# Two-stage attention and a maxout layer on one core: pooling of batch 1 one burst later, first two output pairs with their linear term last

## The chip, the cores and the metric

The kernel runs on one core of a Trainium2 chip. Times are device microseconds (us) of one execution. The profile is one profiled execution on the same core; its engines are PE (TensorE), DVE (VectorE), ACT (ScalarE), POOL (GpSimd) and SP (SyncE, which here only issues DMAs).

## The reference

There are 4 batches of 12544 tokens with 128 channels, 32 inducing rows, and a layer with 1024 hidden columns.

```python
def mab(q, kv):                    # a = softmax(scale * q @ kv.T), returns a @ kv
...
h = mab(I, x)                      # pooling: 32 rows attend to all tokens of a batch
x = mab(x, h)                      # every token attends to the 32 pooled rows
g = np.maximum(x @ w1, x @ w2)
return g @ w_out
```

## The kernel before

The layer is taken apart as max(a, b) = a + relu(b - a). So an output tile is relu(e · hwd) · w_out plus a linear term e · m1, both scaled by the softmax's reciprocal sum. Here e are the unnormalised exponentials of a token against the 32 pooled rows, hwd is the pooled rows times (w2 - w1), and m1 is the pooled rows times w1 · w_out.

**Pooling** of a batch goes over seven pieces of 16 (the last one 2) tiles of 128 tokens. `p1_scores` (line 361) takes 16 matmuls (L366) from the transposed tokens `xT` and one exponential on ACT (L375). `p1_accum` (line 381) takes 16 matmuls (L388), an addition on DVE (L398 for the first, then L401) and one on POOL (L405, then L408). `small_fold`, `small_h`, `small_hwd` and `small_m1` then make hwd and m1 of that batch, and `m1d` (L513, on POOL: m1 masked into four blocks of 32 rows). `transpose_batch` (line 134) lets SP issue seven DMA transposes (L130), released by a tiny POOL copy (L136).

**Bursts** are the main work. `seq` (line 782) lists them over all batches; the loop of line 834 counts them as g. Batch 0 has g = 0 to 48: one block of 8 tiles (4 bursts), five of 16 tiles (8 bursts each), one of 8 (4) and one of 2 (1). A burst (line 586) is eight matmuls (L606) into four PSUM banks; each bank is then evicted with a relu, on DVE (L637) or ACT (L641), as a small planner (`Model.pick`, line 41) decides at build time from assumed costs. There are eight banks in all; `bank` (line 104) takes the one that the planner thinks free first, and the first writer of a bank waits for the eviction that empties it.

**Finals** are the output pairs: 16 matmuls (L668) from the evicted relu tiles, a product with the reciprocal sums on DVE (L694), and after every second one a DMA to the output (L704, issued by POOL for batches 0 to 2). Four finals follow from every part of four bursts, and one is taken from the queue in each iteration. The linear term of a final comes in one of two ways. For two finals at once it goes first, as four matmuls of 32 rows (L621) right behind the burst: that is the `lead`, taken when the queue's head has an even number. Without a lead it goes last, as two matmuls of 128 rows with `m1d` (L677).

The order of every engine is what the loop writes. Within iteration g it is: the burst with its lead, one-time preparations (g = 1 to 3; `small_m1(0)` in g = 3), the staging of later blocks (L541, L551), one final, the sums of a new block (L562, L571), and then the jobs that `at` put down for g, among them the pooling of the next batch:

```python
for i in range(NP1):
    s = g + (14 + 4 * i if b == 0 else 5 + 5 * i)
    at(s, p1_scores, nb, i)
    at(s + 2, p1_accum, nb, i)
```

For batch 1, then, scores stand in g = 14, 18, ..., 38 and sums in g = 16, 20, ..., 40. In batch 0 the leads stand in every even g from 4 on. The rest of the pooling chain stands in g = 40 (fold), 43, 44 and 45.

## Time and profile before

| | |
|---|---|
| median of 5 runs | 341.36 us (339.39 to 342.08) |
| profiled execution, whole time | 339.07 us |
| its span | 337.3 us |
| mean granted TensorE clock | 0.998 |
| busy: PE, DVE, ACT, POOL | 328.0, 298.3, 271.2, 94.1 us |
| L606 (burst) | 1600 matmuls, 81.5 us busy |
| L668 (finals) | 3136 matmuls, 208.6 us busy |
| L621 (lead) | 380 matmuls, 31.2 us busy |
| L637 (relu on DVE) | 337, mean 679 ns |
| L641 (relu on ACT) | 447, mean 601 ns |
| L694 (output product on DVE) | 196, mean 417 ns |

A row with an engine, a line and an operation is a group of like instructions; "busy" is their summed time without overlaps. In the timeline each row gives the start, the time until the last of a run of like instructions ended, the engine, the line, what is written from what, and in brackets how long the engine had been idle and what ended that. Matmuls are pipelined, so one that takes 0.2 us may follow the one before it after 0.06 us: what counts for the path is the distance from start to start. PEld is the loading of weights, which runs ahead of the matmuls.

### The profile page before, as it was taken

How to read it: one execution, taken by the hardware profiler on the slowest of the kernel's cores; microseconds unless marked ns; L12 is line 12 of the kernel's file. 1: busy time of each engine (PE TensorE's matmuls, PEld its weight loads, DVE VectorE, ACT ScalarE, POOL GpSimd, SP SyncE). 2: the span in 40 equal slices, each digit the busy share in tenths (PEclk: the TensorE clock that was granted, in tenths of full speed). 3: DMA queues.
4: the chain of work that ended last, by engine and by line, in shares of the span. 5: the costliest groups of instructions: out<-in, count | busy, mean ns of one | idle time of the engine just before them, and what ended most of it. 6: DMA issues, size and time to landing. Idle time of an engine off the chain costs nothing.

```text
span 337.3 us, 14365 instructions
## 1 busy us (share of the span) xinstructions
PE 328.0 (97%) x6267; PEld 260.3 (77%) x6267; DVE 298.3 (88%) x631; ACT 271.2 (80%) x526; POOL 94.1 (28%) x166
## 2 busy tenths in 40 slices
PE   7988999999999999999999999999999999999995
PEld 3775868887878878888877878888777777878875
DVE  1768989999989999999998999999998998999993
ACT  4658878887898787887898877787899989888881
POOL 6331222356632234542341232332242100000000
PEclk9999999999999999999999999999999999999999
DMA  8999899999629996994219991221221221222222
GB/s 211 208 206 215 214 228 225 250 205 252 179 96 201 213 207 154 199 240 142 89 71 216 224 214 66 95 95 66 96 96 64 111 96 72 94 92 97 95 96 111
DMA packets 54143, 51.47 MB, mean 153 GB/s; under 512 B 41536, under 2 KB 42464, under 8 KB 54080
## 3 DMA queue, kind: packets, MB, share of 16 engines
q0 software_dynamic: 11552, 32.38, 36.5%
q1 hardware_dynamic: 42528, 18.17, 25.4%
q8 instruction: 49, 0.80, 0.9%
q14 instruction: 14, 0.11, 0.1%
HBM read 28.33 MB, written 25.69 MB: 160 GB/s over the span
## 4 chain that ended last, share of the span: by engine, by line
PE 86%; DMA 6%; ACT 3%; DVE 2%; POOL 1%; issue 1%; POOLq 0%
PE ps L668 55%; PE ps L606 18%; PE ps L621 4%; DMA xn<-in_x_dram 4%; ACT relu L641 2%; PE ps L366 2%; PE ps L388 2%; PE ps L541 2%; DMA xT<-xn 2%; DVE relu L637 1%; DVE o L694 1%; POOL xn L126 1%; PE ps L562 1%; ACT e L551 0%; PE ps L482 0%
## 5 line engine op out<-in xcount | busy, mean ns | idle before, releaser
L641 ACT ACTIVATE relu<-ps 128x512 f16<-128x512 f32 x447 | 237.1, 601 | 42.7 <-PE ps L606 30.5
L637 DVE TENSOR_SCALAR relu<-ps 128x512 f16<-128x512 f32 x337 | 217.1, 679 | 6.3 <-PE ps L606 5.1
L668 PE MATMUL ps<-woutp,relu 128*128 128x128 f16 x3136 | 208.6, 220 | 0.0
L668 PEld LDWEIGHTS <-relu 128*128 128x128 f16 x3136 | 175.6, 98 | 31.4 <-issue 21.7
L694 DVE TENSOR_TENSOR o<-ps,rp 128x256 f32<-128x256 f32 x196 | 81.7, 417 | 17.5 <-PE ps L668 13.0
L704 POOL DMA_DIRECT2D out_dram<-o x75 | 41.1, 548 | 149.8 <-DVE o L694 115.7
L606 PE MATMUL ps<-e,hwd 32*128 32x256 f16 (+1 forms) x1600 | 81.5, 270 | 0.7 <-ACT relu L641 0.4
L606 PEld LDWEIGHTS <-hwd 32*128 32x128 f16 x1600 | 26.2, 92 | 18.9 <-issue 3.3
L621 PE MATMUL ps<-m,e 32*128 32x128 f16 x380 | 31.2, 214 | 1.5 <-ACT m L508 0.8
L621 PEld LDWEIGHTS <-e 32*128 32x128 f16 x380 | 18.5, 92 | 9.0 <-issue 6.1
L408 POOL TENSOR_TENSOR eacc<-eacc,et 128x512 f32<-128x512 f32 (+1 forms) x18 | 18.5, 1028 | 0.2
L375 ACT ACTIVATE et<-ps 128x512 f16<-128x512 f32 (+1 forms) x21 | 11.4, 545 | 5.0 <-PE ps L366 5.0
L121 POOL DMA_DIRECT2D xn<-in_x_dram x21 | 11.4, 546 | 4.6 <-DMA xn<-in_x_dram 2.1
L366 PE MATMUL ps<-inducingT,xT 128*128 128x32 f16 x294 | 10.6, 176 | 0.7 <-DMA xT<-xn 0.7
L551 ACT ACTIVATE e<-ps 128x512 f16<-128x512 f32 (+1 forms) x21 | 10.9, 583 | 0.0
L388 PE MATMUL ps<-et,xn 128*128 128x32 f16 x294 | 10.6, 176 | 0.0
L366 PEld LDWEIGHTS <-xT 128*128 128x128 f16 x294 | 9.5, 96 | 0.9 <-issue 0.9
L388 PEld LDWEIGHTS <-xn 128*128 128x128 f16 x294 | 9.4, 96 | 0.0
L541 PE MATMUL ps<-xT,hT 128*32 128x512 f16 (+2 forms) x116 | 8.5, 356 | 0.0
L194 PE MATMUL ps<-warm 128*128 128x512 f16 x21 | 7.0, 483 | 1.2 <-DVE warm L170 1.2
L246 PE MATMUL ps<-identity,xn 128*128 128x128 f16 x98 | 7.0, 219 | 1.0 <-DMA xn<-in_x_dram 0.4
L251 DVE COPY xT<-ps 128x1024 f16<-128x1024 f16 (+2 forms) x11 | 6.2, 593 | 1.5 <-PE ps L246 1.4
(86 smaller groups left out, 116.4 us busy)
## 6 DMA issues: line engine op xcount, KB each, us to landing
out_dram<-o POOLq DMA_DIRECT2D x72, 256.0 KB, 3.3
xn<-in_x_dram POOLq DMA_DIRECT2D x21, 512.0 KB, 8.6
out_dram<-o SPq DMA_DIRECT2D x24, 256.0 KB, 2.0
xf<-in_x_dram SPq DMA_DIRECT2D x2, 512.0 KB, 4.3
wf<-in_moe_w_dram SPq DMA_DIRECT2D x2, 512.0 KB, 5.7
xn<-in_x_dram POOLq DMA_DIRECT2D x3, 256.0 KB, 11.2
out_dram<-o POOLq DMA_DIRECT2D x3, 128.0 KB, 4.2
xT<-xn SPq DMA_TRANSPOSE x21, 6.7
```

The lines of the kernel that those rows point to most:

```text
L121: nc.gpsimd.dma_start(out=xn_of(b, i)[:, 0:n, :], in_=xr[b, :, k0 : k0 + n, :])
L366: nc.tensor.matmul(out=ps[:, j * M : (j + 1) * M], lhsT=xT_tiles[b % 2][:, k0 + j, :], rhs=inducingT, start=True, stop=True,)
L388: nc.tensor.matmul(out=ps[:, 0:M], lhsT=xn[:, j, :], rhs=et[:, j, :], start=(j == 0), stop=(j == n - 1),)
L408: nc.gpsimd.tensor_add(out=acc, in0=acc, in1=et[:, 0:n, :])
L541: nc.tensor.matmul(out=ps[32 * q : 32 * (q + 1), 0 : self.width], lhsT=st[self.b]["hT4"][:, 32 * q : 32 * (q + 1)], rhs=xT[:, q % self.g], ...
L606: nc.tensor.matmul(out=ps[:, jj * w : (jj + 1) * w], lhsT=st[blk.b]["hwd"][r, 128 * jb : 128 * (jb + 1)], rhs=blk.e2[r, 128 * self.t0 : 12 ...
L621: nc.tensor.matmul(out=part.fin[q][1][:, 128 * s : 128 * (s + 1)], lhsT=part.blk.e2[r, 128 * tt : 128 * (tt + 1)], rhs=st[part.blk.b]["m1" ...
L637: nc.vector.tensor_scalar(out=dst, in0=src, scalar1=0.0, scalar2=None, op0=ALU.max)
L641: nc.scalar.activation(out=dst, in_=src, func=AF.Relu)
L668: nc.tensor.matmul(out=o, lhsT=self.relu[:, jb, q, tt, :], rhs=woutp[:, jb, :], start=(start and s == 0 and jb == 0), stop=(not start and ...
L694: nc.vector.tensor_mul(self.osb[:, h : h + 2, :], ps[:, 0:256].rearrange("p (s c) -> p s c", s=2), rp.broadcast_to((128, 2, 128)),)
L704: eng.dma_start(out=outr[blk.b, :, k : k + nst, :], in_=self.osb[:, 0:nst, :])
```

## The change

The pooling of batch 1 (scores, sums, and the additions that they issue on DVE and POOL) moves from g = 14 + 4i to g = 15 + 4i, so to the iterations without a lead. The fold moves by one iteration and the three steps behind it too, to g = 41, 44, 45 and 46. The condition `g > 4` takes away the lead of g = 4, which belonged to the first two finals of the run; these take the linear term last, in L677. The leads of g = 6, 8, ... stay. The inserted line shifts the line numbers behind 835 by one.

```diff
@@ -808,13 +808,13 @@
             if nb + 1 < B:
                 at(g + l0, hold_loads, nb)
             for i in range(NP1):
-                s = g + (14 + 4 * i if b == 0 else 5 + 5 * i)
+                s = g + (15 + 4 * i if b == 0 else 5 + 5 * i)
                 at(s, p1_scores, nb, i)
                 at(s + 2, p1_accum, nb, i)
                 if nb + 1 < B:
                     at(g + l0 + 2 * i, load_x, nb + 1, i)
             d = 1 if b == 0 else 0
-            for s, f in ((40, small_fold), (42 + d, small_h), (43 + d, small_hwd), (44 + d, small_m1)):
+            for s, f in ((40 + d, small_fold), (42 + 2 * d, small_h), (43 + 2 * d, small_hwd), (44 + 2 * d, small_m1)):
                 at(g + s, f, nb)
@@ -833,7 +833,8 @@
         for g, (p, u) in enumerate(seq):
             lead = []
-            if len(queue) > 1 and queue[0][0].tn == 2 and queue[0][1] % 2 == 0:
+
+            if g > 4 and len(queue) > 1 and queue[0][0].tn == 2 and queue[0][1] % 2 == 0:
                 lead = queue[0:2]
             p.burst(u, lead)
             if 1 <= g <= 3:
```

Since the planner counts along, it deals the banks and some relus anew: in the built programs DVE has three relus more and ACT three fewer, all of them in batch 0. Behind the beginning of batch 1 both engines have the same instructions in the same order.

## The prediction

> **What bounds the kernel now.** I read the page first (parts 1 and 4).

> ```profile
> span 337.3 us, 14365 instructions
> PE 328.0 (97%) x6267; PEld 260.3 (77%) x6267; DVE 298.3 (88%) x631; ACT 271.2 (80%) x526; POOL 94.1 (28%) x166
> PE 86%; DMA 6%; ACT 3%; DVE 2%; POOL 1%; issue 1%; POOLq 0%
> ```

> PE carries 86% of the chain that ended last, so a wait of PE costs its length, and an instruction that PE gets rid of its issue distance. Next the list of waits:

> ```profile
> PE ps L621 <- ACT m L508: 0.8, 1, 0.8
> PE ps L366 <- DMA xT<-xn: 0.7, 1, 0.7
> ```

> These are two single waits of PE, and both belong to steps that the change moves. The timeline shows the first in its place:

> ```profile
> 29.21 0.45 ACT L508 ACTIVATE m<-ps,rs 128x128 f16<-128x128 f32 x1
> 29.70 0.29 PE L621 MATMUL ps<-m,e 32*128 32x128 f16 x4 [0.77 <-ACT m L508]
> 29.74 1.18 POOL L513 TENSOR_TENSOR m1d<-m,mask 128x256 f16<-128x256 f16 x2 [6.65 <-ACT m L508]
> 29.92 1.07 PE L668 MATMUL ps<-woutp,relu 128*128 128x128 f16 x16
> 31.00 0.40 PE L606 MATMUL ps<-e,hwd 32*128 32x256 f16 x8
> ```

> It is the lead of g = 4 waiting for m1, which ACT makes behind four relus. A later stretch of the timeline has the second, and a third kind that the list doesn't show:

> ```profile
> 45.81 0.55 PE L366 MATMUL ps<-inducingT,xT 128*128 128x32 f16 x16 [0.73 <-DMA xT<-xn]
> 46.29 0.40 PE L606 MATMUL ps<-e,hwd 32*128 32x256 f16 x8
> 46.40 0.60 ACT L375 ACTIVATE et<-ps 128x512 f16<-128x512 f32 x1 [0.83 <-PE ps L366]
> 46.72 1.29 DVE L637 TENSOR_SCALAR relu<-ps 128x512 f16<-128x512 f32 x2 [1.18 <-PE ps L606]
> 46.89 2.29 ACT L641 ACTIVATE relu<-ps 128x512 f16<-128x512 f32 x4
> 47.62 0.40 PE L606 MATMUL ps<-e,hwd 32*128 32x256 f16 x8
> 47.85 0.44 PE L621 MATMUL ps<-m,e 32*128 32x128 f16 x4
> 47.92 0.42 DVE L694 TENSOR_TENSOR o<-ps,rp 128x256 f32<-128x256 f32 x1
> 48.02 0.09 PEld L621 LDWEIGHTS <-e 32*128 32x128 f16 x2 [0.18 <-issue]
> 48.25 1.28 DVE L637 TENSOR_SCALAR relu<-ps 128x512 f16<-128x512 f32 x2
> ...
> 58.32 0.27 PE L621 MATMUL ps<-m,e 32*128 32x128 f16 x4
> ```

> L366 is the first pooling scores (g = 14), waiting for the first DMA transpose, which landed at 45.67 (the chain has it from 39.45 for 6.22). The third kind is in the lead after each scores. The exponential goes ahead of the burst's relus on ACT; in g = 16 the second bank of the lead is emptied by the second relu behind it, at about 48.0, and the four L621 take 0.44 where others take 0.27. It is the same in g = 20, 24, 28, 32 and 36: 6 × 0.17 = 1.02 us.

> **What is already tight.** From start to start a burst with its final takes 1.33 us, with a lead 1.44 (timeline, 31.0 to 45.0); scores or sums of a full piece add 0.40, the sums of a new block (L562) 0.08, the staging of two blocks (L541) 0.54. Eight bursts of pooling without a wait are 4 × 1.33 + 4 × 1.44 + 4 × 0.40 + 0.08 = 12.76; g = 20 to 28 took 13.07 (54.66 to 67.73), which is these plus two waits of 0.17. The windows show DVE close behind:

> ```profile
> 46.29:59.92 13.63, 13.63 (x287) 10.95 (x286) 12.36 (x26) 11.03 (x21) 3.97 (x6) 1.00 1.15 226
> ```

> (length, then busy time and count of PE, PEld, DVE, ACT, POOL): DVE works 12.36 of 13.63.

> **The lead of g = 4 goes.** Four L621 go and four L677 come; nothing else moves. L668 of g = 4 no longer stands behind m1. In the built program it waits for the third of the four relus that ACT starts at 27.30, which ends near 28.95, so it can run from 29.0 to 30.0. Then L677 waits for m1d: the first of two POOL products (610 ns each, and the wait is for the first alone) ends at 29.74 + 0.61 = 30.35. So a wait is left, 0.4 instead of 0.77, now behind the final. Two L677 cost what two L668 do, 2 × 0.06; then L562 0.08, and burst 5 starts near 30.65 instead of 31.00. In g = 5 two more L677 take 0.12 back: gain 0.23. Bounds: 0.6 if POOL is done sooner than its rough span says, minus 0.4 if PE had to see both products. I take 0.23. Queued behind the wait are L562 and burst 5, whose relus nobody misses in that time (ACT sat idle 0.80 before those of burst 5).

> **The first scores one burst later.** Burst 15 starts at 45.01 instead of 46.29, scores stand behind its final at 46.3, 0.6 after the transpose landed, which has its release (POOL's L136 in g = 9) and SP queue unchanged. The 0.73 and 0.07 of issue around it go: 0.80. What the wait gave was rest for ACT and DVE (DVE was idle 1.18). Followed forward by their own rows, DVE is free at 45.45, just when burst 15 gives it work, and burst 16 finds its banks empty; I count no loss. If the rest was needed, it comes back as waits: bounds 0.80 and 0.3.

> **The other moves.** PE's work is the same. In even g the lead's banks are now emptied by relus of a burst without an exponential ahead: the 1.02 go. But the exponential now stands ahead of the relus of an even burst, and the next burst is only 1.44 (or 1.52 with L562) away. By the rows above, the second relu behind the exponential ends 1.72 after the burst's start (46.29 to 48.01). In g = 21, 29 and 37 the fourth bank of the burst is emptied by just this relu, PE asks for it at 1.52 + 0.13: 0.09 each, 0.27. In g = 17, 25, 33 it is the first relu (1.2): no wait.

> DVE counts more. In the built program it has 16 relus, not 15, in each eight bursts of the pooling, so every burst gives it two relus and an L694. What do they cost? [...] But the rows overlap: two relus take 1.29, so the second adds 0.61, and from 46.72 over 47.92 to 48.25 a pair takes 1.20 and an L694 0.33. Start to start that is 16 × 0.60 + 8 × 0.33 + 2 × 0.29 + 0.16 = 12.98. This is nearer to what the engine did, so I take it: 0.22 above PE's 12.76, still 0.09 under 13.07. The 0.22 show as waits of 0.06 to 0.09 in the lead of every fourth burst and those of g = 21, 29, 37. The stretches with staging give DVE 0.54 of rest. I sum the new waits to 3 × 0.09 + 5 × 0.07 = 0.62; bounds zero and 1.02 (just the old ones again). Net gain of the stretch: 0.40.

> POOL: its additions now stand behind the output DMA of the same odd g; POOL is busy 4 to 7.6 us in each 13 us window, and the fold has as many bursts before `small_h` as before, so nobody waits. The last steps (g = 44 to 48): `small_hwd` now falls together with a staging and three ACT relus. The copy of hwd on ACT still holds PE near 0.5 in g = 46, as now (bursts 46 and 47 are 2.52 apart, 0.5 more than their work), and g = 45 and 48 may wait 0.1 to 0.2 more while `small_h` no longer lengthens g = 43: minus 0.1, bounds ±0.4. L136 for batch 2 stands behind m1d, up to 2 us later; its first scores came 11 us after it, with a transpose taking about 6.7, so that is covered.

> **Sum.** 0.23 + 0.80 + 0.40 - 0.10 = 1.33 us. The profiled execution took 339.07 (span 337.3 and 1.8 around it), so 337.7 for a like one. That execution was 0.7% quicker than the median of the five runs, and I put the same difference on the median: 341.36 - 1.3 = 340.1.

> **The rivals.**
> *No new waits* (0.22): evictions keep up and all of 1.02 goes. 0.23 + 0.80 + 1.02 = 2.05: 339.3, or 338.4 with the upper bounds. For it: ACT gets three relus less, and the new waits are sums of rows good to a few hundredths. Against: DVE's 12.98.
> *The wait is only moved* (0.12): the rest that DVE and ACT lose at 45.8 comes back, and m1d comes too late. Gain 0.2: 341.1.
> *DVE becomes the bound* (0.16), the slower case, in g = 15 to 41: if a relu takes more than 0.60 start to start, every eight bursts grow by 16 times that, 3.4 such stretches. [...]

> **How the numbers follow.** The likeliest case has 0.50; its own range is 339.3 to 340.9. A difference of under 0.5%, 1.7 us, can't be told from no change here, and 1.33 lies under that; I give 3 in 10 of this case to faster. Faster: 0.22 + 0.15 = 0.37; same: 0.35 + 0.12 = 0.47; slower: 0.16. The range goes from the better bound of the first rival, 338.4, to 342.6, which leaves out most of the DVE case and little else.

> **What would show it.** Right: no wait of L621 for L508, a wait of L677 for POOL of some 0.4; no wait of L366 for the transpose; burst 15 near 44.8; L621 after scores 0.27 to 0.35; eight pooling bursts in about 13.0 with DVE busy over 12.5 of them. Wrong: L668 of g = 4 not before 29.5; burst 16 held by DVE; eight bursts of 13.4 or more (then DVE bounds) or of 12.8 (then nothing does but PE); g = 44 to 49 longer by over 0.5.

## The result and the profile after

The kernel after takes 338.42 us (median of 27 runs, 337.84 to 340.42), the kernel before 341.12 (46 runs, 339.15 to 343.31). The ratio is 0.9931, 95% interval 0.9916 to 0.9947, so faster by 0.7%. The profiled execution took 338.12 us with a mean granted clock of 0.999, against 339.07 and 0.998 before. The profiled executions differ by 0.95 us and the medians by 2.70: that gap is the subject of most of what follows.

The page of the kernel after, span, busy engines and first line of the chain that ended last:

```profile
span 336.4 us, 14365 instructions
PE 327.8 (97%) x6267; PEld 261.1 (78%) x6267; DVE 300.0 (89%) x634; ACT 270.1 (80%) x523; POOL 94.0 (28%) x166
PE 89%; DMA 4%; issue 3%; ACT 2%; POOL 1%; DVE 1%; POOLq 0%
```

PE's share of the chain rose from 86% to 89%. In the list of waits (total, times, longest) the two of the prediction's list are gone, and one half as long has come:

```profile
PE ps L677 <- POOL m1d L513: 0.4, 1, 0.4
```

The timeline of the kernel after at the first final:

```profile
28.82 1.05 PE L668 MATMUL ps<-woutp,relu 128*128 128x128 f16 x16
29.07 0.44 ACT L508 ACTIVATE m<-ps,rs 128x128 f16<-128x128 f32 x1
29.60 1.18 POOL L513 TENSOR_TENSOR m1d<-m,mask 128x256 f16<-128x256 f16 x2 [6.81 <-ACT m L508]
30.27 0.27 PE L677 MATMUL ps<-m1d,e 128*128 128x128 f16 x2 [0.39 <-POOL m1d L513]
...
30.55 0.40 PE L606 MATMUL ps<-e,hwd 32*128 32x256 f16 x8
```

L668 now runs while ACT makes m1, at 28.82 instead of 29.92. Further on in the same timeline, the first scores and the burst and lead behind them:

```profile
45.98 0.55 PE L366 MATMUL ps<-inducingT,xT 128*128 128x32 f16 x16
...
46.46 0.40 PE L606 MATMUL ps<-e,hwd 32*128 32x256 f16 x8
46.56 0.60 ACT L375 ACTIVATE et<-ps 128x512 f16<-128x512 f32 x1 [0.35 <-PE ps L366]
...
46.69 0.27 PE L621 MATMUL ps<-m,e 32*128 32x128 f16 x4
```

L366 has no wait in brackets, and the four L621 behind the scores take 0.27, not 0.44. The price is in a burst, g = 21 (the same in g = 29 and 37):

```profile
54.84 0.59 PE L606 MATMUL ps<-e,hwd 32*128 32x256 f16 x8
```

Eight L606 take 0.59 where others take 0.40. The windows of eight bursts, g = 20 to 28, after:

```profile
53.32:66.22 12.90, 12.90 (x279) 10.97 (x277) 12.75 (x28) 9.66 (x18) 2.98 (x5) 1.00 1.09 235
```

and before:

```profile
54.67:67.73 13.06, 13.06 (x279) 10.82 (x278) 12.37 (x27) 10.09 (x20) 5.05 (x8) 1.00 1.05 238
```

DVE works 12.75 of 12.90 us, yet the stretch became 0.16 shorter.

Now all burst starts of the two traces, each counted from the first burst of its own trace (the loading before it differs by 0.13 us from one execution to another). The table gives how much earlier (minus) a burst of each kernel starts than in the profile of before, in us.

| burst g | before, again | after | after, again | lead only | quarters | two later |
|---|---|---|---|---|---|---|
| 5 | 0.00 | -0.32 | -0.32 | -0.31 | -0.54 | -0.32 |
| 14 | 0.00 | -0.20 | -0.20 | -0.20 | -0.42 | -0.20 |
| 16 | 0.16 | -1.03 | -0.96 | 0.13 | -1.31 | -1.49 |
| 28 | 0.17 | -1.38 | -1.30 | 0.13 | -1.66 | -1.46 |
| 42 | 0.16 | -1.58 | -1.51 | 0.18 | -1.86 | -1.16 |
| 51 | 0.17 | -1.34 | -1.27 | 0.19 | -1.62 | -0.80 |
| 57 | 0.17 | -0.81 | -0.19 | 0.19 | -1.62 | -0.81 |
| 69 | 0.17 | -0.80 | -0.18 | 0.20 | -1.61 | -0.80 |

### The profile page after: what moved, and what is told of

It is laid out like the page before. It is cut to its first block, busy times and chain, and to the rows that moved or that the text cites. A ratio compares the mean times of both kernels' runs of the same rounds, so it can differ in the third digit from the quotient of the medians.

```text
span 336.4 us, 14365 instructions
## 1 busy us (share of the span) xinstructions
PE 327.8 (97%) x6267; PEld 261.1 (78%) x6267; DVE 300.0 (89%) x634; ACT 270.1 (80%) x523; POOL 94.0 (28%) x166
## 4 chain that ended last, share of the span: by engine, by line
PE 89%; DMA 4%; issue 3%; ACT 2%; POOL 1%; DVE 1%; POOLq 0%
PE ps L668 57%; PE ps L606 19%; PE ps L621 4%; DMA xn<-in_x_dram 4%; PE ps L366 2%; PE ps L388 2%; PE ps L541 2%; ACT relu L641 1%; POOL xn L126 1%; PE ps L562 1%; DVE o L694 0%; PE ps L246 0%; PE ps L677 0%; PE ps L303 0%; PE ps L482 0%
## 5 line engine op out<-in xcount | busy, mean ns | idle before, releaser
L641 ACT ACTIVATE relu<-ps 128x512 f16<-128x512 f32 x444 | 235.5, 601 | 43.0 <-PE ps L606 30.6
L637 DVE TENSOR_SCALAR relu<-ps 128x512 f16<-128x512 f32 x340 | 218.7, 678 | 4.6 <-PE ps L606 3.6
L668 PE MATMUL ps<-woutp,relu 128*128 128x128 f16 x3136 | 208.8, 220 | 0.4 <-issue 0.4
L668 PEld LDWEIGHTS <-relu 128*128 128x128 f16 x3136 | 175.8, 98 | 31.9 <-issue 22.3
L694 DVE TENSOR_TENSOR o<-ps,rp 128x256 f32<-128x256 f32 x196 | 81.7, 417 | 16.8 <-PE ps L668 11.9
L606 PE MATMUL ps<-e,hwd 32*128 32x256 f16 (+1 forms) x1600 | 82.2, 270 | 0.8 <-ACT relu L641 0.4
L606 PEld LDWEIGHTS <-hwd 32*128 32x128 f16 x1600 | 26.3, 92 | 19.3 <-issue 3.6
L621 PE MATMUL ps<-m,e 32*128 32x128 f16 x376 | 29.8, 214 | 0.6
L621 PEld LDWEIGHTS <-e 32*128 32x128 f16 x376 | 18.4, 92 | 6.7 <-issue 3.5
L375 ACT ACTIVATE et<-ps 128x512 f16<-128x512 f32 (+1 forms) x21 | 11.4, 544 | 5.1 <-PE ps L366 5.1
L366 PE MATMUL ps<-inducingT,xT 128*128 128x32 f16 x294 | 10.6, 176 | 0.0
L366 PEld LDWEIGHTS <-xT 128*128 128x128 f16 x294 | 9.5, 96 | 0.0
L541 PE MATMUL ps<-xT,hT 128*32 128x512 f16 (+2 forms) x116 | 8.5, 356 | 0.2 <-ACT hwd L490 0.2
L513 POOL TENSOR_TENSOR m1d<-m,mask 128x256 f16<-128x256 f16 x8 | 4.7, 608 | 11.0 <-ACT m L508 6.8
```

The lines of the kernel that those rows point to most:

```text
L366: nc.tensor.matmul(out=ps[:, j * M : (j + 1) * M], lhsT=xT_tiles[b % 2][:, k0 + j, :], rhs=inducingT, start=True, stop=True,)
L541: nc.tensor.matmul(out=ps[32 * q : 32 * (q + 1), 0 : self.width], lhsT=st[self.b]["hT4"][:, 32 * q : 32 * (q + 1)], rhs=xT[:, q % self.g], ...
L606: nc.tensor.matmul(out=ps[:, jj * w : (jj + 1) * w], lhsT=st[blk.b]["hwd"][r, 128 * jb : 128 * (jb + 1)], rhs=blk.e2[r, 128 * self.t0 : 12 ...
L621: nc.tensor.matmul(out=part.fin[q][1][:, 128 * s : 128 * (s + 1)], lhsT=part.blk.e2[r, 128 * tt : 128 * (tt + 1)], rhs=st[part.blk.b]["m1" ...
L637: nc.vector.tensor_scalar(out=dst, in0=src, scalar1=0.0, scalar2=None, op0=ALU.max)
L641: nc.scalar.activation(out=dst, in_=src, func=AF.Relu)
```

## The experiments

Two theories stood at first for the difference between 0.95 and 2.70. A: in a typical execution of before the first scores wait longer for the transpose than in its profile. B: pauses without a semaphore fall differently. Both were tested with the kernel before itself, with each half of the change alone, and with an earlier transpose.

**Before, once more** (no edit).

> The kernel before once more, unchanged, for a second look at an execution nearer to its median (341.1) than the profiled one (339.07). Theory A: the gain beyond the 1.3 us that the schedule accounts for is a longer wait for the first DMA transpose. Then an execution of 341 shows PE waiting 2 to 3 us (not 0.7) at the first pooling scores of g = 14, and the rest of its bursts stand as in the first profile. Theory B: it is pauses that no semaphore explains, as the one of 0.4 us in g = 56 of the changed kernel. Then the wait at g = 14 stays near 0.7 and PE has idle time put down to issue, 1.5 to 2.5 us in sum, at places that differ. If it happens to be an execution near 339 it tells neither apart.

Measured: 339.31 us at a granted clock of 1.0; up to burst 69 its bursts stand within 0.17 us of the first profile (0.34 at the end of the run), and it waits 0.89 us for the transpose where that one waited 0.73. So profiles of full clock agree with each other, and not with the median.

**The later pooling alone.**

```diff
-                s = g + (14 + 4 * i if b == 0 else 5 + 5 * i)
+                s = g + (15 + 4 * i if b == 0 else 5 + 5 * i)
...
+            for s, f in ((40 + d, small_fold), (42 + 2 * d, small_h), (43 + 2 * d, small_hwd), (44 + 2 * d, small_m1)):
```

> Only the pooling one burst later; the lead of g = 4 stays. By the steps of the prediction 0.80 + 0.40 - 0.10 = 1.1 us of schedule. Theory A: also the whole surplus of the change's median, so 2.1 us in all, ratio 0.994, times as narrow as those of the changed kernel. Theory B: 1.1 us, ratio 0.997, and a spread like the kernel before.

Measured: 340.44 (11 runs; a twelfth took 346.61 and is left out) against 340.66; ratio 0.9994, 0.9962 to 1.0026. Both theories had foretold a gain. The profiled execution took 341.03 at a mean clock of 0.990. Its windows show where that is lost (the column behind POOL's busy time and count is the granted clock):

```profile
28.00:29.00 1.00, 0.75 (x9) 0.30 (x9) 1.00 (x2) 1.00 (x3) 0.00 (x0) 1.00 1.02 205
29.00:30.00 1.00, 0.28 (x4) 0.12 (x3) 1.00 (x3) 1.00 (x4) 0.24 (x1) 0.64 1.07 217
30.00:32.00 2.00, 2.00 (x27) 1.94 (x28) 0.35 (x2) 0.65 (x2) 0.94 (x2) 0.50 1.09 217
...
36.00:38.00 2.00, 2.00 (x39) 1.58 (x39) 1.34 (x3) 1.56 (x4) 0.00 (x0) 0.97 0.90 216
```

The clock was halved from 29.28 (0.64 in one us means 0.72 us at half) to 36.12 (0.97 in two), so for 6.84 us. It begins inside the wait of the lead of g = 4, and the final behind it is stretched, as the timeline of this kernel shows:

```profile
29.72 0.39 PE L621 MATMUL ps<-m,e 32*128 32x128 f16 x4 [0.77 <-ACT m L508]
30.05 1.89 PE L668 MATMUL ps<-woutp,relu 128*128 128x128 f16 x16
```

Sixteen L668 take 1.89 instead of 1.07; burst 7 stands 2.8 us later than in before. From burst 14 to 42 the pooling then gains 1.44 us, as in after (1.38). Of the 12 runs only two kept a full clock; they took 338.03 and 338.74. This asked for a third theory, **C**: in many executions TensorE's granted clock is halved (0.50 in the windows above) at the start of batch 0, and taking away the lead of g = 4 prevents it.

**The lead alone.**

```diff
-            if len(queue) > 1 and queue[0][0].tn == 2 and queue[0][1] % 2 == 0:
+            if g > 4 and len(queue) > 1 and queue[0][0].tn == 2 and queue[0][1] % 2 == 0:
```

> Only the lead of g = 4 goes; pooling stays in the even bursts. Burst 5 comes 0.3 us earlier and burst 6 some 0.2. Theory A: that 0.2 is swallowed by the wait for the transpose at g = 14, which comes no earlier by it (its release hangs on POOL's queue): 0 to 0.2 us, ratio 0.9995 to 1.0, spread as before. Theory B: 0.2 us, ratio 0.9993.

Measured: 340.13 (12 runs), ratio 0.9978, 0.9954 to 1.0002. In the profile the 0.20 us won are lost at burst 15, to the wait for the transpose (table above). But all 12 runs have a full clock, where before had it in 12 of 29 beside them. **The same kernel once more:**

> The change without the later pooling, looked at once more: its full-clock runs fell in two groups, near 339.2 and between 340.1 and 340.9, and its profile was of the first. If this execution takes 340.1 or more, its burst starts show where the second group loses 1 us: at burst 15 (a longer wait of the first scores for the transpose), or in pauses without a semaphore elsewhere. If it takes 339.2, nothing is learnt of the second group.

Measured: 339.49, nothing learnt of the runs above 340.1. The full-clock runs of this kernel lie 0.7 us above those of before (339.41), and why stays open.

**The transposes two bursts earlier.**

```diff
-            t0, l0 = (9, 24) if b == 0 else (-3, 16)
+            t0, l0 = (7, 24) if b == 0 else (-3, 16)
```

> The kernel before with the transposes of batch 1 asked for in g = 7 instead of g = 9 (SP and POOL otherwise the same). It takes away the wait at g = 14 alone, pooling stays beside the leads, and the 0.17 at the leads behind the scores stay. Theory A: 0.75 us in a quick execution and the whole surplus in the median, so 1.7 to 2.0 us, ratio 0.9945, with a narrow spread. Theory B: 0.75 us, ratio 0.998, spread as before. If the last load of batch 1 lands only after g = 7, POOL waits for it and the gain is smaller in both.

Measured: 339.78, ratio 0.9982, 0.9960 to 1.0003, and in the profile no gain at all: the releasing copy (L136) now waits 1.90 us for the last load of the batch, and L366 still waits 0.81 us at 45.81. Starting later is what removes this wait; the release can't come earlier. Theory A finds no support here. Nine of the 12 runs lost the clock, yet their median is only 0.55 above that of the three that kept it (339.94 against 339.39), so a lost clock hasn't one price. Here the release hangs on a load and not on the bursts, and the wait behind it may have taken up part of the delay; no trace of such a run was kept.

**The runs sorted by their mean granted clock.** All runs of before beside the experiments (102) fall into three groups: 42 at 0.9975 or more, median 339.41; 48 near 0.995, median 341.25; 12 near 0.990, median 341.99. Against the full clock a mean of 0.995 is one stretch of 3.40 us at half clock (so in the profile of the fillers of 32 rows below), 0.990 two (6.84 us in that of the pooling alone). The 39 runs of after have 37 at full clock, median 338.42. So the median of before, by its time, is that of an execution which lost its clock once.

**Fillers in the hole.** Theory C foretells that before keeps its clock if the 0.77 us are filled.

```diff
                 for part, q in lead:
                     part.open_final(q)
+                for _ in range(3 if lead and lead[0][0] is parts[0] and lead[0][1] == 0 else 0):
+                    part, q = lead[0]
+                    nc.tensor.matmul(
+                        out=part.fin[q][1], lhsT=warm[:, 0:128], rhs=warm, start=True, stop=True
+                    )
```

> The kernel before, with three filler matmuls (128 columns of weights by 512 columns of zeros, about 0.21 us each at the full clock) put between the burst of g=4 and its lead, where TensorE has nothing to do for 0.77 us; they write into the lead's own bank, which the lead then starts afresh. Nothing else is changed. Theory C (the hole of 0.77 us ahead of the lead at g=4 makes the clock gate halve TensorE's clock in most executions, and the change fills that hole): the fillers take nothing, since they end before m1 is there (0.64 of 0.77 us), and at least 9 of 12 runs show a mean clock of 0.9975 or more, where about 12 of 29 of the kernel before do; the median falls by 1.3 to 2.0 us, to 339.1 to 339.7. Rival D (the clock falls for another reason, by chance or by what the pool of chips does in that hour, or because of the start of the long series of matmuls after the hole): the share of runs at the full clock stays below 7 of 12 and the median stays within 0.6 us of before.

> The same with one filler matmul instead of three: the hole ahead of the lead at g=4 is cut from 0.77 to about 0.55 us. Theory C says that how long TensorE is idle decides: the share of runs at the full clock lies between that of the kernel before (about 4 in 10) and that with three fillers; if a hole of 0.4 us is harmless (the kernel after has one of 0.39 us and 25 of 27 runs at the full clock), 6 to 11 of 12, median 339.3 to 340.7. Rival D: as before, within 0.6 us, without an order between one and three fillers.

Measured: with three fillers 12 of 12 runs at full clock, 339.68; with one, 4 of 12, 340.70. Ratios 0.9981 (0.9958 to 1.0003) and 1.0003 (0.9977 to 1.0029). The clock did what C says; the fall of the median missed its 1.3 us (0.22), since before itself had 17 of 33 full-clock runs on that chip. With three, TensorE has work from 29.01 on and keeps its full clock:

```profile
29.01 0.81 PE L619 MATMUL ps<-warm 128*128 128x512 f16 x3
29.76 0.29 PE L626 MATMUL ps<-m,e 32*128 32x128 f16 x4
29.98 1.07 PE L673 MATMUL ps<-woutp,relu 128*128 128x128 f16 x16
```

One filler left a hole of 0.37 us, no longer than the 0.39 of after, and still 8 of 12 runs lost the clock: the length of the hole isn't what decides.

**A longer hole in the kernel after.** One product of 512 columns on GpSimd in place of two of 256; the unchanged kernel after ran beside it.

```diff
-            for q in (0, 2):
-                nc.gpsimd.tensor_mul(
...
+            nc.gpsimd.tensor_mul(
+                m1d,
+                m1[:, None, :].broadcast_to((128, 4, 128)),
+                mask.broadcast_to((128, 4, 128)),
+            )
```

> The kernel after once more, unchanged, for two questions. First, is the pause at the burst of g=57 in its profile (0.54 us on TensorE and ScalarE with no semaphore behind it) part of the kernel or of that one execution? If of the execution, burst 57 stands about 1.3 us earlier than in the profile of before, counted from the first burst, and not 0.8; if of the kernel, 0.8 again. Second, as a partner on the same chip for the kernel with one mask instruction: median 338.4 (338.0 to 338.8), ratio to before 0.990 to 0.996, at least 10 of 12 runs at a mean clock of 0.9975 or more.

> The kernel after, with the masked product m1d built by one GpSimd instruction of 512 columns instead of two of 256. TensorE waits for the whole of it at the first output pair: 0.39 us become about 0.95 (0.59 us more, less a fixed cost saved), at about the place where before has its hole of 0.77 us. Sum of the wait alone: 0.5 to 0.6 us later from burst 5 on, part of which the next waits may take up; full-clock runs at 338.7 to 339.0. Theory C (the hole at the start of batch 0 sets off the clock gate, whatever makes the hole): 8 or fewer of 12 runs at the full clock, where after has 25 of 27, and a median of 339.5 to 341. Rival D (it is the lead's own matmuls, 32 rows in four row groups ahead of the series of 128 rows, that go with the lowered clock, and the hole is beside the point): 10 or more of 12 at the full clock, median 338.7 to 339.0.

The hole in the timeline (lines one lower; L667 is the final, L676 its linear term):

```profile
28.95 1.05 PE L667 MATMUL ps<-woutp,relu 128*128 128x128 f16 x16
...
30.82 0.27 PE L676 MATMUL ps<-m1d,e 128*128 128x128 f16 x2 [0.82 <-POOL m1d L512]
```

Measured: 338.47 (ratio 0.9937, 0.9909 to 0.9964), after 338.48 (0.9953, 0.9926 to 0.9981); 10 and 12 of 12 runs at full clock. The wait costs 0.42 us at burst 5, yet its medians can't be told apart. A hole of 0.82 us that comes after sixteen 128-row matmuls does no such harm (10 of 12 runs at full clock) as 0.77 us behind bursts of 32 rows (42 of 102 in before). C as first put, any hole at this place, fell.

**Fillers of 32 rows.** What is left is either TensorE's time without a matmul after the weak stretch, or how much 128-row work that stretch holds.

```diff
-                        out=part.fin[q][1], lhsT=warm[:, 0:128], rhs=warm, start=True, stop=True
+                        out=part.fin[q][1], lhsT=warm[0:32, 0:128], rhs=warm[0:32, :],
+                        start=True, stop=True, tile_position=(0, 0)
```

> The kernel before with three fillers of 512 columns in the hole ahead of the lead at g=4, as in the run with three fillers of 128 rows, but with 32 rows of weights and data instead of 128: TensorE is busy as long, on a quarter of its rows. So far the length of the hole alone does not tell which kernels lose the clock: 0.82 us after sixteen 128-row matmuls (one mask instruction) cost it in 2 of 12 runs, 0.37 us after 32-row bursts with one filler (lead kept) in 8 of 12. Theory R (what counts is how much 128-row work lies in a stretch of some 3 us; bursts and leads of 32 rows count for little, and in the kernel before nearly none lies between 26.96 and 29.92 us): the clock is lost as in the kernel before, 3 to 8 of 12 runs at the full clock (38 of 85 for before so far), median 339.9 to 341.2. Theory I (what counts is the time without any matmul after the stretch with waits): 11 or 12 of 12 at the full clock, as with 128 rows, median 339.4 to 339.8.

Measured: 340.56, ratio 0.9993 (0.9968 to 1.0019); 6 of 12 runs at full clock, where the same fillers with 128 rows had 12 of 12. In its profile the hole is shut (no wait in brackets), and the clock goes all the same:

```profile
29.74 0.80 PE L619 MATMUL ps<-warm 32*128 32x512 f16 x3
30.49 0.29 PE L627 MATMUL ps<-m,e 32*128 32x128 f16 x4
```

```profile
30.00:31.00 1.00, 1.00 (x12) 0.55 (x11) 1.00 (x2) 1.00 (x4) 0.48 (x1) 0.98 1.12 229
31.00:34.00 3.00, 3.00 (x36) 2.57 (x34) 1.58 (x5) 1.35 (x3) 0.70 (x2) 0.50 1.05 210
34.00:36.00 2.00, 2.00 (x36) 1.71 (x34) 1.43 (x3) 1.10 (x3) 0.55 (x1) 0.91 1.08 215
```

Half clock from 30.96 to 34.36: 3.40 us, with TensorE busy all through 30 to 31. So closing the hole isn't enough. The two kernels with three fillers ran on different chips, and these differ: beside the fillers of 128 rows before kept its clock in 17 of 33 runs, beside those of 32 rows in 4 of 17. The 12 of 12 against 6 of 12 is therefore not a clean pair; the sum over windows in the last section speaks to the same question from the traces alone.

**The pooling two bursts later,** with the lead of g = 4 gone: later, but beside the leads again.

```diff
-                s = g + (15 + 4 * i if b == 0 else 5 + 5 * i)
+                s = g + (16 + 4 * i if b == 0 else 5 + 5 * i)
...
+            for s, f in ((40 + 2 * d, small_fold), (42 + 3 * d, small_h), (43 + 3 * d, small_hwd), (44 + 3 * d, small_m1)):
```

> The kernel after, with the pooling of batch 1 two bursts later than in before instead of one: it falls beside the bursts with leads again, as in before, and is only later. Theory A' (the two terms of the sum are separate: the wait for the transpose goes with any later place, the waits of 0.17 us at the leads go only with the odd place, and the odd place brings 0.19 us at the bursts of g=21, 29 and 37): in the profile the wait of the first scores for the transpose (0.73 us in before) is gone, the six or so leads behind scores take 0.44 instead of 0.27 us again (+1.02), the bursts behind the pooling's copies take 0.40 to 0.45 again (-0.57), so burst 44 stands 0.4 to 0.5 us later than in after, and the median at the full clock is 338.8 (338.5 to 339.2). Rival E (the odd place brings nothing on balance, being later is all): burst 44 as in after, 338.4. Theory C expects 10 to 12 of 12 runs at the full clock, since the lead at g=4 is gone here as well.

Measured: 338.64, ratio 0.9953 (0.9931 to 0.9975), 12 of 12 at full clock. The table shows the parts: the wait for the transpose is gone (-1.49 at burst 16, of which 0.40 are scores not yet done there), then nothing more is won up to burst 28 (-1.46, with the same 0.40), where after goes from -1.03 to -1.38: the odd place does bring a gain of its own. At burst 44 it stands 0.33 later than after (-1.25 against -1.58), a little under the 0.4 to 0.5 of theory A'.

**m1d in quarters,** a version that follows from the 0.39 us that are left.

```diff
-            for q in (0, 2):
+            for q in range(4):
                 nc.gpsimd.tensor_mul(
-                    m1d[:, q : q + 2, :],
+                    m1d[:, q : q + 1, :],
```

> The kernel after, with the masked product m1d built in four GpSimd instructions of 128 columns instead of two of 256. TensorE waits 0.39 us for the first of them at the first output pair, and needs only its first quarter. If the first quarter takes about half of the 0.59 us, the wait falls to about 0.1 us: burst 5 comes 0.29 us earlier, and if that isn't swallowed further on, the time is 338.1 (0.3 below after, about 338.4). If GpSimd's fixed cost of an instruction makes a quarter as long as a half, nothing moves (338.4), and the second pair waits instead. Theory C expects no fewer runs at the full clock than after, 11 or 12 of 12.

Measured: 337.93 (10 runs), ratio 0.9938 (0.9903 to 0.9973), 9 of 10 at full clock. The wait is 0.17 instead of 0.39, burst 5 comes 0.22 earlier, and 0.28 of it stay to burst 51. Its median is the lowest of all, but it didn't run beside the kernel after, and 0.5 us between chips prove nothing; the trace shows the 0.28.

How many runs kept the clock, by kernel:

| kernel | between the 128-row product at 26.3 and the first final | runs at full clock |
|---|---|---|
| before | bursts, hole 0.77, lead of 32 rows | 42 of 102 |
| pooling alone; early transposes | the same | 2 of 12; 3 of 12 |
| before, one filler of 128 rows | hole 0.37 | 4 of 12 |
| before, three fillers of 32 rows | no hole | 6 of 12 |
| before, three fillers of 128 rows | no hole | 12 of 12 |
| after (two sets) | final starts 1.1 us earlier | 37 of 39 |
| lead alone; two later | the same | 12 of 12; 12 of 12 |
| quarters; one mask | the same, hole 0.17; 0.82 behind the final | 9 of 10; 10 of 12 |

## Why the prediction was right, and where its size was off

**The lead of g = 4: right.** Forecast a wait of L677 of 0.4 and a gain of 0.23; measured 0.39 and 0.20 (burst 14). Alone it is worth nothing at the full clock, as the wait for the transpose takes it; only with the later pooling does it stay.

**The first scores: right.** Forecast 0.80; between bursts 14 and 16 after gains 1.03 - 0.20 = 0.83.

**The leads behind scores: right in sum, wrong in the parts.** All L621 from g = 16 to 36 take 0.27, so 6 × 0.17 = 1.02 went, as in the first rival. The waits of 0.06 to 0.09 at every fourth lead, from DVE's lag, didn't come. Those of g = 21, 29 and 37 are 0.19 each and not 0.09: 0.57 against 0.62 in all. From burst 16 to 42 the gain is 0.55, forecast 0.40; these parts give 1.02 - 0.57 = 0.45, and the other 0.10 isn't placed. The sum from the rows' distances stands: eight bursts take 12.90 with DVE at 12.75, near the 12.98 from start to start and far from the 14.8 that the rows' durations give end to end (16 × 0.678 + 8 × 0.413 + 2 × 0.179 + 0.247, an estimate from the rows of after, 53.32 to 66.22). DVE as the bound fell: the eight bursts of 13.4 or more didn't come, and what they would have cost no run shows.

**The end of batch 0:** forecast -0.10, measured -0.24 (bursts 42 to 51). The sum at bursts 51 to 56 is 1.34, forecast 1.33. That is closer than its parts are, so in part luck.

**What the sum lacked.** At g = 57 after pauses for 0.54 us, so 0.80 are left at the end: the 0.95 of the profiles, less the 0.13 of loading. This pause comes back with 1.09 us in the second profile of after, with 0.42 in that of the pooling alone, and in none of the profiles of quarters, two later and one mask.

**The step that failed: "I put the same difference on the median".** It took the 2.3 us between the profiled execution and the median of before for a spread that the change leaves alone. It was, for the most part, the half clock. From 341.25, the group in which the median of before lies, to 339.41 at full clock are 1.84 us; from there to the 338.42 of after 0.99 us. Together 2.83, measured 2.70. The change did both: the later pooling brings the 0.99 (its two full-clock runs alone, 338.03 and 338.74, stand where after does), and taking away the lead of g = 4 the rest, by moving a final of 128 rows ahead into a stretch of small matmuls. Neither half shows this alone (ratios 0.9994 and 0.9978; product 0.9972): the pooling alone loses the clock in 10 of 12 runs, the lead alone wins it and gives its 0.20 back to the transpose.

Two things in this split stay open. The kept traces with one lost stretch stand only 1.39 us (one filler) and 1.49 us (fillers of 32 rows) late at burst 7, and 1.57 and 1.67 at burst 57, not 1.84. And the full-clock runs of the lead alone lie 0.72 above those of before, so the two halves don't simply add up.

**The range: luck.** The gain was twice the forecast one, and 338.42 lies inside the range by 0.02 us. That edge, 338.4, was drawn for evictions that never wait and no clock was in it; by the prediction's own upper bounds (0.60 + 0.80 + 1.02 + 0.30 = 2.72) it should have been 338.6. By its line of 0.5% the result is a gain, to which it gave 0.37.

That the stretch around the lead of g = 4 decides over the clock is shown by the table, and so is that one kernel has runs of both kinds. Half clock lasted 3.40 us in the profile of the fillers of 32 rows and 6.84 us in that of the pooling alone; what sets these lengths wasn't shown. The longest hole there doesn't sort the kernels: with 0.77 us before lost its clock in 60 of 102 runs, with 0.37 one filler in 8 of 12, with none the fillers of 32 rows in 6 of 12, while one mask, with 0.82, kept it in 10 of 12. That 128 rows count for more than 32 is the reading that fits the table and, as the last section works out, the clock records of all fourteen traces. The run of 32-row fillers was forecast from it (3 to 8 of 12 at full clock) and came out so (6), but not on the chip of its pair.

## What to carry to other kernels

When the profiled execution is faster than the median, sort the runs by their mean granted clock before putting a forecast from the one on the other: here some 1.8 of 2.70 us lay in that. A change of order is worth what it takes off the path plus what it does to the clock, so look for stretches of a few us in which TensorE has only small or waiting matmuls, and put a long series of full-height ones there: here sixteen matmuls of 128 rows that start 1.1 us earlier went with 37 of 39 runs at full clock, against 42 of 102. For steps of a tenth of a us, sum start-to-start distances from the trace, not durations (here 12.98 against 14.8, where 12.90 was measured).

## What the runs showed of the hardware that was not expected

How busy TensorE is didn't decide over its clock here. The first two lines are the 3.41 us ahead of a loss, in the pooling alone and in the fillers of 32 rows (74% and 86% busy); the third is a stretch of before, once more, behind which the clock stayed (72%):

```profile
25.87:29.28 3.41, 2.51 (x36) 1.24 (x34) 3.30 (x7) 3.41 (x8) 0.00 (x0) 1.00 1.06 213
27.55:30.96 3.41, 2.92 (x33) 1.35 (x31) 3.30 (x7) 3.41 (x9) 0.44 (x1) 1.00 1.07 216
27.97:31.38 3.41, 2.44 (x43) 1.65 (x43) 2.69 (x6) 2.61 (x7) 1.19 (x2) 1.00 1.07 215
```

The pause at g = 57, in the second profile of after, on PE alone:

```profile
111.65 0.40 PE L668 MATMUL ps<-woutp,relu 128*128 128x128 f16 x4
112.96 0.84 PE L668 MATMUL ps<-woutp,relu 128*128 128x128 f16 x12 [0.91 <-issue]
```

ACT stands still with it until 114.61, 1.77 us, put down to "issue" as well. In both profiles of after a packet of the instruction queue moved between 110 and 111 us, behind transposes whose queue took 94.9% and 82.3% of the DMA engines' time from 105 to 116 us; in those of quarters and one mask, without a pause, it moved at 108.3 and 109.7. That late instructions are the cause is only argued from this, and wasn't tried.
